# Zero blocks, unread products and small copies moved inside a fused attention and expert kernel

## The chip, the core and the metric

The kernel runs on one core of a Trainium2 chip. The metric is the time of one execution on the device in microseconds (us). Five engines work side by side, each with its own instruction queue in program order: TensorE (PE; its weight loads are listed as PEld), VectorE (DVE), ScalarE (ACT), GpSimd (POOL) and SyncE (SP, which here only issues transfers). They wait for one another and for the transfers (DMA) through semaphores. TensorE writes its results to PSUM, the other tiles lie in SBUF, inputs and outputs in DRAM. The instruction order on each engine is fixed by the order in the source.

## The reference

Two parts, one after the other. First, attention for 8 batches and 8 heads of 64 channels, with 512 local and 32 global tokens: a global token attends to everything, a local token to the 32 global tokens and to the local tokens at most 32 positions away. Then the 8 x 544 = 4352 rows of 512 channels go to a layer of 8 experts, each of which takes at most 80 rows:

```python
logits = x @ w_gate                                   # 4352 x 8
expert_idx = np.argmax(logits, axis=1)
probs = softmax(logits);  gate_w = probs[rows, expert_idx]
out = zeros((4352, 512))
for e in range(8):
    tok_idx = np.where(expert_idx == e)[0]
    if len(tok_idx) > 80:
        tok_idx = the 80 of them with the largest gate_w
    h = np.maximum(x[tok_idx] @ w1[e], 0.0)           # 512 -> 1024
    out[tok_idx] = gate_w[tok_idx, None] * (h @ w2[e])  # 1024 -> 512
```

At most 640 of the 4352 output rows differ from zero, so the kernel writes zeros over the whole output and then scatters the experts' rows into it.

## The kernel before

Attention goes in 16 steps q = 0 to 15, each with four heads of one batch. A step prepares its successors: the loads of step q+4, the casts of q+3, the transposes of q+2, and the scores of q+1. `...` marks cuts; the line numbers in the profile are those of the kernel before.

```python
def T_chunk(q, t, cp=None):                       # transposes of q (t = 0) or k (t = 1)
    T_ps = psT([P, 8, 2, 64], FP16, ...)          # PSUM, two tiles with tag T
    ...                                           # 8 transposes (L299)
    nc.scalar.copy(out=dst, in_=src)              # L307: qkT <- T_ps

def qw_copy(q):                                   # L311: the first 32 queries once more behind the 512,
    nc.vector.tensor_copy(out=qkT[q % 2][:, :, 512:544], in_=qkT[q % 2][:, :, 0:32])

def G_fill(q):                                    # which only this product reads
    g_ps = psS(...)                               # PSUM, two tiles with tag S
    ...  nc.tensor.matmul(..., rhs=qkT[q % 2][:, j, 32:544], ...)

def L_fill(q, j):                                 # local scores: L353, L362 on TensorE
    l_ps = [psS([P, 512], FP32, ...) for hh in range(2)]
    ...
    nc.scalar.activation(out=eL[:], in_=l_ps[hh][:], func=AF.Exp, scale=scale)   # L367

def H_chunk(q, h):                                # weighted values of head h (L409)
    ...
    if h % 2:                                     # the norm of two heads
        nc.vector.reciprocal(out=rec[:], in_=o2[:, :, :, 64])                    # L416
        nc.vector.tensor_tensor(out=s["xn"]..., in0=o2..., in1=rec..., op=ALU.mult)  # L417

def X_chunk(q, j): ...                            # transposes of xn (L447), copy of them to xT (L451, L453)
```

The experts' limit of 80 needs a top-80 per expert. The scores are sorted in groups of batches, 8 values in a step of MAX8 (L580) and MATCH_REPLACE8 (L582) on VectorE. The steps wait in a list `work`; `some(n)` emits n of them, and NS gives how many at three places of step q:

```python
NS = [[1, 1, 1]] * 7 + [[1, 1, 2], [1, 1, 0], [1, 2, 1], [1, 1, 1], [2, 2, 2], [1, 1, 0], [2, 2, 3], [1, 1, 0],
                        [0, 0, 0]]

def zeros(n):                                     # L638: n of 17 blocks of 128 x 1024 zeros to the output
    for _ in range(n):
        if nz[0] < 17:
            nc.sync.dma_start(out=out_z[nz[0]], in_=zt[:]); nz[0] += 1

def warm(n):                                      # n products that nobody reads (L651)
    w_ps = psS([P, 512], FP32, "w_ps")
    for _ in range(n):
        nc.tensor.matmul(out=w_ps[:], lhsT=onesb[:], rhs=w1sb[0][:, 0, 0:512], start=True, stop=True)

for q in range(NQ):
    if 0 < q and q + 4 < NQ: load_qk(q + 4)       # SyncE
    if not first and q + 2 < NQ: load_v(q + 2)    # SyncE
    ...
    G_chunk(q); G_all(q); H_chunk(q, 0); Q_chunk(q)
    T_chunk(q + 2, 0)
    ...
    L_fill(q + 1, 0); mask(q + 1, 0)
    ...                                           # La(pend), regroup(q + 3, 0)
    some(NS[q][0])
    H_chunk(q, 1)
    qw_copy(q + 2)
    ...                                           # Lb1(pend): logits of the batch that is done
    some(NS[q][1])
    L_fill(q + 1, 1)
    T_chunk(q + 2, 1); kO_copy(q + 2)
    H_chunk(q, 2)
    ...                                           # mask(q + 1, 1), Lm(pend), Lb2(pend), Ld(late)
    G_fill(q + 1); Q_fill(q + 1, 0)
    ...                                           # regroup(q + 3, 1)
    H_chunk(q, 3)
    X_chunk(q, 0); Q_fill(q + 1, 1); ...; X_chunk(q, 1)
    some(NS[q][2])
    for i in range(*WS[q:q + 2]): load_w(...)     # expert weights, issued by GpSimd
zeros(4)
...                                               # the last batch's gates, the last steps of the top-80
zeros(17)                                         # the rest: 13 blocks
warm(60)
```

`Ld` writes the normalised rows of a batch to a scratch tensor in DRAM (x_scr), as bf16 pairs with the gate behind them. The end of the kernel finds the row numbers of each expert (idx), gathers the rows, and runs the experts:

```python
nc.vector.tensor_tensor(out=idx[:], ...)                          # L903
for e in range(E):
    nc.gpsimd.indirect_dma_start(out=xg[e][:], in_=x_dram.ap(), ...idx[:, e:e + 1]...)   # L907
load_w(NRES + 3, (2, 3)); load_w(NRES + 4, (0, 1, 2, 3))          # the last weights
warm(16)

def fy(e):
    ...                                                           # y_ps: output products (L936)
    nc.vector.tensor_scalar(out=y[:, 0:DF // 2], in0=y_ps[:, 0:DF // 2], scalar1=g, ...)      # L940
    nc.scalar.activation(out=y[:, DF // 2:], in_=y_ps[:, DF // 2:], func=AF.Copy, scale=g)    # L941
    nc.gpsimd.indirect_dma_start(out=out, ...idx[:, e:e + 1]..., in_=y[:], ...)               # L943

fx(0)                                             # transposes of the gathered rows (L918, L921)
for e in range(E):
    if e + 1 < E: fx(e + 1)
    fh(e)                                         # hidden products (L929), relu on ScalarE (L931)
    if e: fy(e - 1)
fy(E - 1)
```

A scatter waits for every zero block, since both write the output. SyncE issues its transfers in order, and each waits for the one eight places before it.

The softmax here doesn't subtract the row's maximum and nothing guards it: scores larger than these inputs give would overflow.

## Time and profile before

The median of three runs is 263.44 us (263.38 to 263.84).

| | busy us of 263.6 | instructions |
|---|---|---|
| TensorE products | 226.8 | 4025 |
| TensorE weight loads | 157.0 | 4025 |
| GpSimd | 162.0 | 245 |
| VectorE | 158.1 | 462 |
| ScalarE | 135.0 | 237 |

| transfer | count | KB each | us from issue to landing (median) |
|---|---|---|---|
| zero blocks (L638) | 17 | 512 | 11.6 |
| q, k (L156) | 16 + 16 | 512 | 5.7, 5.2 |
| v (L214) | 16 | 512 | 6.6 |
| rows to x_scr (L567) | 8 | 385.5 | 11.4 |

The profile of one execution lists for each instruction when it ran and what ended the idle time before it, in the form `[idle <-releaser]`. Its slices give the granted TensorE clock (PEclk, 1.00 is full speed) and the share of time in which the 16 DMA engines were busy. A chain follows the work that ended last back to the start; "issue" is time in which an engine waited for nothing that the profile shows. Where an engine waits for several semaphores, the profile names the one that came last by its own reckoning, which can be the wrong one. Attention takes the time up to about 186 us, and the end of the kernel, from the last batch's gates to the last scatter, the rest.

### The profile page before, as it was taken

The numbers are of one execution on the slowest core, as the hardware profiler recorded it, in microseconds if no ns is written. First come the engines' busy times: TensorE is split into PE (matmuls) and PEld (weight loads), VectorE is DVE, ScalarE is ACT, GpSimd is POOL, SyncE is SP. The second block draws the span as 40 slices with busy tenths as digits, with TensorE's granted clock in tenths as the row PEclk, the third lists the DMA queues.
The fourth block names the chain that finished last, engine by engine and source line by source line (L and its number), as shares of the span: only waits on it lengthen the run. The fifth ranks groups of instructions, "written<-read, shape, count | busy, mean of one in ns | idle before, by whom it ended". The sixth has DMA issues, their size and how long they took to land.

```text
span 263.6 us, 9572 instructions
## 1 busy us (share of the span) xinstructions
PE 226.8 (86%) x4025; PEld 157.0 (60%) x4025; DVE 158.1 (60%) x462; ACT 135.0 (51%) x237; POOL 162.0 (61%) x245
## 2 busy tenths in 40 slices
PE   6887899999999999998998889998959796599990
PEld 2466676776766767666676667766424352477650
DVE  2765545554853888768478687878979880012220
ACT  3657558695695865868569485461230000033420
POOL 2549795787957869569686788986550005832331
PEclk9999999999999999999999999999999999569996
DMA  7999899995998999989998997987999999999921
GB/s 227 245 302 254 267 259 235 285 199 90 252 257 155 261 146 310 194 185 280 171 262 213 213 212 145 204 145 141 262 277 251 223 281 375 417 323 214 242 85 50
DMA packets 67739, 60.05 MB, mean 228 GB/s; under 512 B 46192, under 2 KB 50544, under 8 KB 67696
## 3 DMA queue, kind: packets, MB, share of 16 engines
q1 hardware_dynamic: 59712, 40.61, 53.6%
q0 software_dynamic: 7840, 18.80, 39.1%
q8 instruction: 31, 0.51, 0.8%
q14 instruction: 12, 0.10, 0.1%
q10 hardware_dynamic: 144, 0.03, 0.1%
HBM read 61.57 MB, written 14.70 MB: 289 GB/s over the span
## 4 chain that ended last, share of the span: by engine, by line
PE 36%; DVE 20%; DMA 18%; issue 9%; ACT 5%; POOL 5%; SPq 3%; POOLq 1%; ACTq 0%; DVEq 0%
DMA out_dram<-zt 10%; PE o_ps L409 8%; DMA x_scr<-xgb 6%; PE o_ps L396 5%; DVE xn L417 5%; PE T_ps L299 4%; PE og L432 4%; PE x_ps L447 4%; DVE scT L582 3%; DVE lst L580 3%; ACT qkT L307 2%; ACT eL L367 2%; POOL out_dram L943 2%; PE l_ps L362 2%; PE lt_ps L472 2%
## 5 line engine op out<-in xcount | busy, mean ns | idle before, releaser
L375 POOL TENSOR_TENSOR eL<-eL,band 128x512 f32<-128x512 f32 x30 | 38.1, 1271 | 27.1 <-ACT eL L367 27.0
L307 ACT COPY qkT<-T_ps 128x1024 f16<-128x1024 f16 x31 | 31.5, 1017 | 33.7 <-PE T_ps L299 28.7
L409 PE MATMUL o_ps<-vb,eL 128*64 128x65 f32 x1024 | 43.7, 227 | 0.0
L367 ACT ACTIVATE eL<-l_ps 128x512 f32<-128x512 f32 x64 | 34.9, 599 | 15.2 <-PE l_ps L362 15.2
L409 PEld LDWEIGHTS o_ps<-vb,eL 128*64 128x64 f32 x1024 | 35.0, 137 | 9.8 <-issue 5.9
L165 ACT CAST qkr<-qkb 128x1024 f16<-128x1024 f32 (+1 forms) x26 | 27.3, 1052 | 2.8 <-DMA qkb<-in_q_l_dram 2.5
L931 ACT ACTIVATE fhT<-h_ps 128x320 bf16<-128x320 f32 x16 | 6.5, 431 | 41.5 <-PE xT_ps L918 38.5
L447 PE MATMUL x_ps<-misc,xn 128*128 128x128 f32 x128 | 20.9, 286 | 7.0 <-DVE xn L417 6.0
L651 PE MATMUL w_ps<-w1sb,onesb 128*128 128x512 bf16 x115 | 26.3, 379 | 0.0
L907 POOL DMA_INDIRECT xg<-x_scr,idx x8 | 7.8, 974 | 26.9 <-DMA out_dram<-zt 24.8
L417 DVE TENSOR_TENSOR xn<-o_ps,rec 128x512 f32<-128x512 f32 x32 | 22.1, 692 | 2.1
L299 PE MATMUL T_ps<-ident,qkr 128*128 128x128 f16 x256 | 20.5, 226 | 1.3 <-ACT qkr L165 1.0
L319 POOL COPY kO<-qkT 128x512 f16<-128x512 f16 x31 | 19.9, 642 | 1.9
L416 DVE RECIPROCAL rec<-o_ps 128x8 f32<-128x8 f32 x32 | 6.5, 203 | 23.1 <-PE o_ps L409 23.1
L447 PEld LDWEIGHTS x_ps<-misc,xn 128*128 128x128 f32 x128 | 13.4, 141 | 10.5 <-DVE xn L417 8.4
L458 POOL CAST xb<-xn 128x1024 bf16<-128x1024 f32 x16 | 16.6, 1040 | 3.8 <-DVE xn L417 3.8
L943 POOL DMA_INDIRECT out_dram<-y,idx x8 | 7.4, 928 | 18.2 <-ACT y L941 9.1
L651 PEld LDWEIGHTS <-onesb 128*128 128x128 bf16 x115 | 10.7, 98 | 13.0 <-issue 1.3
L396 PE MATMUL o_ps<-vg,eG 32*128 32x65 f32 x512 | 18.1, 276 | 0.0
L299 PEld LDWEIGHTS <-qkr 128*128 128x128 f16 x256 | 15.2, 100 | 4.3 <-ACT qkr L165 1.9
L226 POOL COPY vb<-vb 64x1040 f32<-64x1040 f32 x16 | 17.0, 1065 | 0.9
L396 PEld LDWEIGHTS o_ps<-vg,eG 32*128 32x128 f32 x512 | 15.8, 186 | 2.3 <-issue 1.5
(155 smaller groups left out, 473.8 us busy)
## 6 DMA issues: line engine op xcount, KB each, us to landing
out_dram<-zt SPq DMA_DIRECT2D x17, 512.0 KB, 11.6
qkb<-in_q_l_dram SPq DMA_DIRECT2D x16, 512.0 KB, 5.7
qkb<-in_k_l_dram SPq DMA_DIRECT2D x16, 512.0 KB, 5.2
vb<-in_v_l_dram SPq DMA_DIRECT2D x16, 512.0 KB, 6.6
w2sb<-in_moe_w_dram POOLq DMA_DIRECT2D x12, 512.0 KB
w1sb<-in_moe_w_dram POOLq DMA_DIRECT2D x10, 512.0 KB
x_scr<-xb SPq DMA_DIRECT2D x8, 385.5 KB, 11.4
vb<-in_moe_w_dram POOLq DMA_DIRECT2D x6, 512.0 KB
```

The source lines that it names most:

```text
L165: cp(out=qkr[q][:, t, i].rearrange("p i g d -> p g i d"), in_=qkb[q % 2][:, t, :, i])
L226: nc.gpsimd.tensor_copy(out=v[64:128, 1], in_=v[64:128, 0])
L299: nc.tensor.transpose(out=T_ps[:, i].rearrange("x a p -> x (a p)"), in_=qkr[q][:, t, i].rearrange("p g d -> p (g d)"), identity=ident16[:, :])
L307: nc.scalar.copy(out=dst, in_=src)
L319: eng.tensor_copy(out=kO[q % 2][:, a], in_=buf[:, 608:1120].rearrange("x (u w y) -> x u w y", w=2, y=64)[:, :, ::-1, :])
L367: nc.scalar.activation(out=eL[:], in_=l_ps[hh][:], func=AF.Exp, scale=scale)
L375: eng.tensor_tensor(out=eL[:], in0=eL[:], in1=band[:].rearrange("p t i -> p (t i)"), op=ALU.mult)
L396: nc.tensor.matmul(out=s["o"][h][:, u, :], lhsT=s["eG"][32 * r:32 * r + 32, 128 * u:128 * u + 128], rhs=vg[b % 2][32 * r:32 * r + 32, qd, ...
L409: nc.tensor.matmul(out=o[64 * odd:64 * odd + 64, u, :], lhsT=s["eL"][h][:, 64 * t:64 * t + 64], rhs=v[:, 16 * odd + 4 * h + u, :], start=F ...
L417: nc.vector.tensor_tensor(out=s["xn"][:, :, 64 * h - 64:64 * h + 64].rearrange("p u (h d) -> p h u d", h=2), in0=o2[:, :, :, 0:64], in1=re ...
L447: nc.tensor.transpose(out=x_ps[:, 128 * u:128 * u + 128], in_=s["xn"][:, u, 128 * j:128 * j + 128], identity=identf[:, :])
L651: nc.tensor.matmul(out=w_ps[:], lhsT=onesb[:], rhs=w1sb[0][:, 0, 0:512], start=True, stop=True)
```

## The change

The change moves small pieces of work, and the result stays the same row by row.

- Six of the 17 zero blocks are issued one at a time at the end of the steps 3, 4, 5, 8, 12 and 13, so that seven instead of thirteen are left for the end.
- The unread products ahead of the first gathered rows become 27 instead of 16. They keep TensorE at work while it waits.
- The copy of the first 32 queries (`qw_copy`) goes from VectorE to ScalarE, and stands directly behind the copy of the transposed q that it reads.
- In the steps 9 and 11 one top-k step goes from the second place to the third, from before the norm of the last two heads to behind it.
- The last expert's y is scaled by VectorE alone, without ScalarE's half.

```diff
     def qw_copy(q):
-        nc.vector.tensor_copy(out=qkT[q % 2][:, :, 512:544], in_=qkT[q % 2][:, :, 0:32])
+        nc.scalar.copy(out=qkT[q % 2][:, :, 512:544], in_=qkT[q % 2][:, :, 0:32])
...
-    NS = [[1, 1, 1]] * 7 + [[1, 1, 2], [1, 1, 0], [1, 2, 1], [1, 1, 1], [2, 2, 2], [1, 1, 0], [2, 2, 3], [1, 1, 0],
+    NS = [[1, 1, 1]] * 7 + [[1, 1, 2], [1, 1, 0], [1, 1, 2], [1, 1, 1], [2, 1, 3], [1, 1, 0], [2, 2, 3], [1, 1, 0],
...
         elif q + 2 < NQ:
             T_chunk(q + 2, 0)
+            qw_copy(q + 2)
...
         H_chunk(q, 1)
-        if not first and q + 2 < NQ:
-            qw_copy(q + 2)
...
+        if q in (3, 4, 5, 8, 12, 13):
+            zeros(1)
         for i in range(*WS[q:q + 2]):
             load_w(i // 4, (i % 4,))
...
-    warm(16)
+    warm(27)
...
-        nc.vector.tensor_scalar(out=y[:, 0:DF // 2], in0=y_ps[:, 0:DF // 2], scalar1=g, scalar2=None, op0=ALU.mult)
-        nc.scalar.activation(out=y[:, DF // 2:], in_=y_ps[:, DF // 2:], func=AF.Copy, scale=g)
+        n = DF if e == E - 1 else DF // 2
+        nc.vector.tensor_scalar(out=y[:, 0:n], in0=y_ps[:, 0:n], scalar1=g, scalar2=None, op0=ALU.mult)
+        if n < DF:
+            nc.scalar.activation(out=y[:, n:], in_=y_ps[:, n:], func=AF.Copy, scale=g)
```

The cuts leave out the calls for the first steps: `qw_copy(1)` and `qw_copy(2)` move behind their transposes in the same way.

## Prediction

> **What bounds the kernel now.** I read the page first (engine shares, slices, chain), then the chain in order of time, then the timeline of the end and of two attention steps, and last the busy times by window.
>
> The page's chain says that no engine holds the whole span: TensorE carries a third, and DMA, mostly the zero blocks, 18%.
>
> ```profile
> ## 4 chain that ended last, share of the span: by engine, by line
> PE 36%; DVE 20%; DMA 18%; issue 9%; ACT 5%; POOL 5%; SPq 3%; POOLq 1%; ACTq 0%; DVEq 0%
> DMA out_dram<-zt 10%; PE o_ps L409 8%; DMA x_scr<-xgb 6%; PE o_ps L396 5%; DVE xn L417 5%; PE T_ps L299 4%; PE og L432 4%; PE x_ps L447 4%; DVE scT L582 3%; DVE lst L580 3%; ACT qkT L307 2%; ACT eL L367 2%; POOL out_dram L943 2%; PE l_ps L362 2%; PE lt_ps L472 2%
> ```
>
> In order of time the zero blocks are one stretch (start, length, what):
>
> ```profile
> 196.95 15.96 DMA x_scr<-xgb
> 212.92 11.57 DMA out_dram<-zt
> 224.51 15.91 DMA out_dram<-zt
> ```
>
> It ends at 240.42, where the first scatter could go. I don't believe this stretch as the cause of the end. The timeline (start, length, engine, line) shows a second path beside it:
>
> ```profile
> 217.96 3.61 PE L651 MATMUL w_ps<-w1sb,onesb 128*128 128x512 bf16 x16
> 218.34 0.16 DVE L903 TENSOR_TENSOR idx<-idf,inv_ps 80x8 uint32<-80x8 f32 x1
> 219.38 1.04 POOL L907 DMA_INDIRECT xg<-x_scr,idx  x1 [24.78 <-DMA out_dram<-zt]
> ...
> 230.74 0.77 ACT L931 ACTIVATE fhT<-h_ps 128x320 bf16<-128x320 f32 x2 [37.48 <-PE xT_ps L918]
> ...
> 256.50 0.48 DVE L940 TENSOR_SCALAR y<-y_ps,xg 80x256 f32<-80x256 f32 x1 [1.25 <-PE y_ps L936]
> 257.01 0.47 ACT L941 ACTIVATE y<-y_ps,xg 80x256 f32<-80x256 f32 x1 [1.26 <-DVE y L940]
> 257.76 0.92 POOL L943 DMA_INDIRECT out_dram<-y,idx  x1 [0.81 <-ACT y L941]
> ```
>
> The indices are ready at 218.50, the first gather starts 0.88 us later, its rows reach TensorE at 225.77, the first expert's y is scaled at 235.96, the eighth at 256.50, and only 0.28 us after the last y the last scatter starts. Scatters that wait for 240.42 then run every 1.27 us against one y in about 3.0 us, so their backlog is gone by 244 to 247. The end hangs on the experts, not on the zeros. And the experts start on a slow TensorE (window, length, busy times, then PEclk, DMA share, GB/s):
>
> ```profile
> 190.00:195.00 5.00, 2.15 (x10) 0.78 (x8) 4.45 (x24) 2.68 (x9) 3.35 (x8) 1.00 1.05 307
> 222.00:226.00 4.00, 0.23 (x4) 0.24 (x4) 0.00 (x0) 0.00 (x0) 3.06 (x4) 0.81 1.03 416
> 226.00:230.00 4.00, 3.06 (x44) 2.76 (x42) 0.65 (x2) 0.00 (x0) 3.39 (x5) 0.50 1.03 417
> 230.00:234.00 4.00, 2.78 (x34) 2.46 (x34) 0.33 (x1) 1.64 (x4) 3.03 (x5) 0.50 1.04 398
> 234.00:238.00 4.00, 4.00 (x48) 2.67 (x47) 0.71 (x2) 1.17 (x3) 0.00 (x0) 0.91 1.09 249
> ```
>
> The 16 unread products end at 221.57, TensorE stands still until 225.77 (4.2 us), and the clock is halved until about 234.7. In 190:195 there is a pause of 2.9 us (192.15 to 195.07) and the clock stays at 1.00.
>
> In attention, two waits matter here. In an odd step (q=11) ScalarE copies the transposed q (L307), then takes the exponentials whose end frees the PSUM tile of the next products (L353); and DVE, late with the top-k step, delays L447:
>
> ```profile
> 138.69 1.01 ACT L307 COPY qkT<-T_ps 128x1024 f16<-128x1024 f16 x1 [2.43 <-PE T_ps L299]
> 139.64 1.09 ACT L367 ACTIVATE eL<-l_ps 128x512 f32<-128x512 f32 x2
> 140.29 0.38 PE L353 MATMUL l_ps<-bandneg,ident 128*128 128x512 f16 x1
> 142.08 0.83 DVE L311 COPY qkT<-qkT 128x64 f16<-128x64 f16 x1
> 145.06 0.69 DVE L417 TENSOR_TENSOR xn<-o_ps,rec 128x512 f32<-128x512 f32 x1
> 145.81 0.65 PE L447 MATMUL x_ps<-misc,xn 128*128 128x128 f32 x4 [1.27 <-DVE xn L417]
> ```
>
> **What the Trainium skill says.** "TensorE: Matmul & The Clock Gate", section "What's actually happening": after at least one idle window of about 3.4 us the clock goes to half, and about 3.4 us of sustained work bring it back; the window runs freely. The trace agrees: 4.2 us of pause gave 0.50, 2.9 us did not. "DMA: Bandwidth & Descriptors", section "Issuing engines are not separate DMA queues": transfers of all issuers interleave on the same 16 engines. The trace agrees: the first gather, 80 rows, took 6.4 us from its start to its use while zeros and weights moved 400 to 417 GB/s. "GPSIMD Engine Reference", section "1. Specifications": its SBUF interface is shared with VectorE, with contention in two-port modes. That fits L311, one small copy that takes between 0.17 and 1.00 us (median 0.375).
>
> **The change, part by part.**
>
> Unread products, 16 to 27. One costs 3.61/16 = 0.226 us, so 27 take 6.1 us and end at 224.06 instead of 221.57 on today's time axis. The pause before 225.77 shrinks from 4.2 to 1.7 us, under the 2.9 us that was harmless, so I expect the clock to stay at 1.00. They don't delay the gathered rows, which come at 225.8 or at best some 1.5 us sooner. At full clock the start of the experts is: products of expert 0 1.31 us, transposes of expert 2 0.31, then the pair "hidden products of expert 1, output of expert 0", which in steady state takes 238.98 - 235.90 = 3.08 us. From 226.63 that is 231.3, against 235.96 now. Gain 4.6 us; I take 4.4.
>
> Six zero blocks moved. Each is 0.524 MB. At 410 GB/s that is 1.28 us, six are 7.7 us of DMA work that leaves the end, so the zeros end near 233 instead of 240. By the argument above this alone doesn't move the end. It may shorten the first gather's 6.4 us; but of the thirteen late blocks it is the last six that go; nine are issued before 220, and seven of them stay, so I take 0.5 us. In attention the blocks meet DMA engines that show a share of 0.92 (60 to 120 us) to 0.97 (120 to 170), but 207 to 213 GB/s against 417 at the end, and loads that land 5.2 to 6.6 us after issue and are read about one step (11 us) later. Cost there: 0.
>
> The last y on VectorE alone. Now 0.48 on DVE and 0.47 on ScalarE one after the other, 256.50 to 257.48. A DVE evacuation of 512 columns from PSUM (L453) takes 0.68. I take 0.73 with the scale: gain 0.25.
>
> The wrap copy on ScalarE. DVE loses 16 copies of 0.375 us. ScalarE gets one between L307 and L367. Its smallest operation in the trace (128x40) takes 0.25 us; it must wait for L307 to end, which costs the 0.08 us by which L367 starts before L307's end now, and 0.04 to start. That shifts L367 by 0.29 us. In odd steps the shift goes straight to L353 (140.29 waits for the first exponential), in even steps to the copy of the logits, for which TensorE waits up to 0.5 us now. Thirteen steps have it: at most 13 x 0.29 = 3.8 us; not every shift will reach the end of its step, I count 8, cost 2.3 us. On DVE the copy is off the path except in q=8, where it holds a PSUM tile back by 0.14 us.
>
> The two top-k steps. In q=9 and q=11 one step of MAX8 and MATCH_REPLACE8 (1.16 and 0.90 us) goes from before the norm of the last heads to behind it. TensorE waits there 1.03 and 1.27 us, where the other steps wait 0.32 to 0.33. The last heads' products end at 121.75 and 143.81; norm (0.2 + 0.7) and starts put L447 at 122.85 and 144.93 instead of 123.51 and 145.81: gains of 0.66 and 0.88.
>
> Sum: 263.44 - 4.4 - 0.5 - 0.25 + 2.3 - 0.14 - 0.66 - 0.88 = 258.9 us.
>
> **Rivals.** (1) The clock falls all the same. For: the window runs freely, transposes and the wait for the second gather follow the unread products, and if the gather is late the pause grows. Against: 1.7 us is far from 3.4. Then only 0.5 + 0.25 + 1.7 - 2.3 remain: 263.3 us. (2) ScalarE becomes the bound of attention: all 13 shifts count, 260.4 us. For: L307, L367, the regrouping casts and L342 run without a gap in an odd step. (3) The wrap copy is absorbed, and freeing DVE and its shared port helps GpSimd too: 256.6 us. For: the spread of L311. Against: GpSimd waits for ScalarE in these steps (27.0 us at L375), not for the port. (4) The zeros delay loads of attention: the blocks stand ahead of loads in SyncE's order, and SyncE has a wait of 1.9 us on such a chain already. Each late load would cost 1 to 3 us: 260 to 264 us. (5) The late weights of experts 6 and 7, issued behind the gathers, become the wait when the experts run 4.6 us sooner. Against: they have no zeros beside them then.
>
> **Range and chances.** The clock term is the surest large one; attention can be off by 2 us either way, and the cadence after y0 holds one irregular step (3.90 against 3.0 us) that I leave as it is. So 258.9 us, 255.5 to 262.3. Two per cent is 258.2, just under my figure: faster by over 2% 0.42, within 2% 0.56, slower 0.02.
>
> **What would show it.** Right: PEclk of 1.00 from the first gathered rows on, the first y about 11.7 us after the first gather starts (16.6 - 4.4 - 0.5) instead of 16.6, the zeros' last landing before the first y. Wrong if: PEclk shows 0.5 there (rival 1); attention ends (the last L417, now 185.03) more than 2.5 us later (2, or 4 if ScalarE's cast L165 waits for DMA) or earlier than now (3); TensorE waits for w1sb or w2sb among the experts (5).

## The result, and the profile after

The changed kernel takes 266.91 us (266.71 to 267.32), against 263.41 us for the kernel before on the same chip: a ratio of 1.0137, interval 1.0112 to 1.0162. It is 3.5 us slower. The prediction was 258.9 us, and its range ended at 262.3.

In the changed kernel all lines behind L844 have moved by two: the gather is L909, the relu L933, y L943 and L945, the scatter L947. Its page gives this chain (shares of the span):

```profile
PE 36%; DMA 22%; ACT 11%; issue 10%; POOL 9%; DVE 6%; SPq 3%; POOLq 1%; ACTq 0%
PE o_ps L409 8%; DMA out_dram<-zt 6%; PE o_ps L396 6%; PE T_ps L299 5%; DMA x_scr<-gate 5%; ACT qkT L307 5%; PE og L432 4%; DMA vg<-in_v_g_dram 4%; ACT eL L367 3%; DMA x_scr<-xb 3%; PE x_ps L447 3%; DVE xn L417 3%; POOL out_dram L947 2%; PE l_ps L362 2%; POOL xg L909 2%
```

VectorE's share has fallen from 20% to 6% and ScalarE's has risen from 5% to 11%, as the moved copy and top-k steps would make it. Two transfers are new among the lines listed, the gate behind the rows of the last batch (x_scr<-gate, 5%) and the values of the global tokens (vg, 4%). In order of time (start, length, what) the first of them stands here:

```profile
188.68 5.04 DMA x_scr<-xgb
193.74 16.95 DMA out_dram<-zt
210.71 12.63 DMA x_scr<-gate
223.58 0.61 issue
```

The gate write of the last batch is issued at 210.71, 22 us after attention's last norm (188.64), where it was 17 us before (202.14 after 185.03); it lands at 223.34, and the first gather starts 1.07 us behind that. The timeline of the end (start, length, engine, line) shows what that costs:

```profile
222.23 0.16 DVE L905 TENSOR_TENSOR idx<-idf,inv_ps 80x8 uint32<-80x8 f32 x1
224.41 1.04 POOL L909 DMA_INDIRECT xg<-x_scr,idx  x1 [26.21 <-DMA out_dram<-zt]
...
230.22 0.32 PE L920 MATMUL xT_ps<-identbf,xg 80*128 80x80 bf16 x4 [2.38 <-DMA xg<-x_scr,idx]
...
231.58 0.45 PE L920 MATMUL xT_ps<-identbf,xg 80*128 80x80 bf16 x4 [1.04 <-DMA xg<-x_scr,idx]
...
233.19 0.44 ACT L933 ACTIVATE fhT<-h_ps 128x320 bf16<-128x320 f32 x1 [36.32 <-PE h_ps L931]
...
258.66 0.75 DVE L943 TENSOR_SCALAR y<-y_ps,xg 80x512 f32<-80x512 f32 x1 [1.25 <-PE y_ps L938]
259.69 0.91 POOL L947 DMA_INDIRECT out_dram<-y,idx  x1 [0.58 <-DVE y L943]
```

The gather starts 2.02 us behind the row numbers instead of 0.88. The pause of TensorE ahead of the first rows is 2.4 us instead of 4.2, and a wait of 1.0 us for the second rows follows. And the clock falls all the same (window, length, busy times, then PEclk, DMA share, GB/s; the first line is the kernel before, the others are the changed one):

```profile
200.00:205.00 5.00, 5.00 (x25) 2.27 (x24) 4.76 (x12) 0.00 (x0) 0.00 (x0) 1.00 1.11 237
...
200.00:205.00 5.00, 5.00 (x18) 1.86 (x16) 4.76 (x14) 0.00 (x0) 0.00 (x0) 0.66 1.06 272
...
226.00:230.00 4.00, 1.84 (x9) 0.63 (x7) 0.00 (x0) 0.00 (x0) 3.08 (x4) 1.00 1.04 421
230.00:234.00 4.00, 2.74 (x41) 2.61 (x42) 0.65 (x2) 0.44 (x1) 3.08 (x4) 0.59 0.72 260
234.00:238.00 4.00, 4.00 (x44) 3.16 (x42) 0.32 (x1) 1.31 (x3) 4.00 (x7) 0.56 0.70 120
```

The first two lines stand behind the pause of 2.9 us for the gates that the prediction used as its measure. In the kernel before it left the clock at 1.00; here the same pause, again 2.92 us, halves it (0.50 from 200 to 203 us).

In attention, ScalarE's timeline of step 11 shows the copy (L311) where the change puts it:

```profile
143.19 1.01 ACT L307 COPY qkT<-T_ps 128x1024 f16<-128x1024 f16 x1 [2.41 <-PE T_ps L299]
144.23 0.24 ACT L311 COPY qkT<-qkT 128x64 f16<-128x64 f16 x1
144.38 1.08 ACT L367 ACTIVATE eL<-l_ps 128x512 f32<-128x512 f32 x2
145.35 1.05 ACT L165 CAST qkr<-qkb 128x1024 f16<-128x1024 f32 x1
```

The exponentials start 1.19 us behind the start of L307, where it was 0.95 before (139.64 - 138.69): 0.24 us later.

Last, SyncE's queue around the block of step 5, first in the changed kernel:

```profile
80.29 5.90 SPq L567 DMA_DIRECT2D x_scr<-xb  x1
...
90.28 0.42 SPq L638 DMA_DIRECT2D out_dram<-zt  x1
92.45 0.39 SPq L156 DMA_DIRECT2D qkb<-in_q_l_dram  x1
94.55 0.38 SPq L156 DMA_DIRECT2D qkb<-in_k_l_dram  x1
95.02 0.43 SPq L214 DMA_DIRECT2D vb<-in_v_l_dram  x1
95.50 4.54 SPq L218 DMA_DIRECT2D vg<-in_v_g_dram  x2
```

and then in the same kernel without the six moved blocks (e7 below):

```profile
86.34 0.63 SPq L214 DMA_DIRECT2D vb<-in_v_l_dram  x1
87.03 8.73 SPq L218 DMA_DIRECT2D vg<-in_v_g_dram  x4
```

A row write alone takes 5.90 us to issue here, but 5.87 us in e7 as well. What differs is the wait for places in the queue: of the 172 transfers in this trace none starts before the one eight places ahead has landed, and the loads at 92.45 and 94.55 start 0.07 us behind two writes of rows (L568 and L569, issued at 86.24 and 86.76) that landed 6.1 and 7.7 us after their issue. So the values are asked for 8.5 us later than without the blocks, though the step itself is only 2.5 us later (start of L396 in step 7: 94.74 against 92.23). They land at 105.28, and TensorE starts step 8 with them at 105.33.

Besides the global scores, which the text above the prediction names alone, the last tile of the local scores (L362) also reads the wrap copy (its columns are 480 to 544). It changes nothing in the argument.

### The profile page after: what moved, and what is told of

Same layout as the page of the kernel before. It is cut to its first block, busy times and chain, and to the rows that moved or that the text cites. A ratio compares the mean times of both kernels' runs of the same rounds, so it can differ in the third digit from the quotient of the medians.

```text
span 265.5 us, 9521 instructions
## 1 busy us (share of the span) xinstructions
PE 232.2 (87%) x4036; PEld 159.9 (60%) x4036; DVE 151.0 (57%) x446; ACT 137.5 (52%) x252; POOL 161.1 (61%) x245
## 4 chain that ended last, share of the span: by engine, by line
PE 36%; DMA 22%; ACT 11%; issue 10%; POOL 9%; DVE 6%; SPq 3%; POOLq 1%; ACTq 0%
PE o_ps L409 8%; DMA out_dram<-zt 6%; PE o_ps L396 6%; PE T_ps L299 5%; DMA x_scr<-gate 5%; ACT qkT L307 5%; PE og L432 4%; DMA vg<-in_v_g_dram 4%; ACT eL L367 3%; DMA x_scr<-xb 3%; PE x_ps L447 3%; DVE xn L417 3%; POOL out_dram L947 2%; PE l_ps L362 2%; POOL xg L909 2%
## 5 line engine op out<-in xcount | busy, mean ns | idle before, releaser
L307 ACT COPY qkT<-T_ps 128x1024 f16<-128x1024 f16 x31 | 31.5, 1017 | 34.5 <-PE T_ps L299 29.3
L409 PE MATMUL o_ps<-vb,eL 128*64 128x65 f32 x1024 | 44.8, 230 | 1.3 <-issue 1.3
L367 ACT ACTIVATE eL<-l_ps 128x512 f32<-128x512 f32 x64 | 34.7, 594 | 17.1 <-PE l_ps L362 17.1
L409 PEld LDWEIGHTS o_ps<-vb,eL 128*64 128x64 f32 x1024 | 35.9, 140 | 11.3 <-issue 7.3
L651 PE MATMUL w_ps<-w1sb,onesb 128*128 128x512 bf16 x126 | 30.4, 396 | 0.0
L933 ACT ACTIVATE fhT<-h_ps 128x320 bf16<-128x320 f32 x16 | 6.7, 430 | 38.4 <-PE h_ps L931 38.4
L909 POOL DMA_INDIRECT xg<-x_scr,idx x8 | 7.8, 972 | 28.3 <-DMA out_dram<-zt 26.2
L299 PE MATMUL T_ps<-ident,qkr 128*128 128x128 f16 x256 | 19.9, 221 | 2.9 <-DVE qkr L165 1.6
L651 PEld LDWEIGHTS <-onesb 128*128 128x128 bf16 x126 | 12.2, 101 | 15.6 <-issue 3.6
L319 POOL COPY kO<-qkT 128x512 f16<-128x512 f16 x31 | 19.1, 616 | 1.9
L396 PE MATMUL o_ps<-vg,eG 32*128 32x65 f32 x512 | 19.1, 282 | 0.1
L458 POOL CAST xb<-xn 128x1024 bf16<-128x1024 f32 x16 | 16.6, 1039 | 3.2 <-DVE scT L582 2.4
L396 PEld LDWEIGHTS o_ps<-vg,eG 32*128 32x128 f32 x512 | 16.9, 191 | 2.5 <-issue 1.5
L299 PEld LDWEIGHTS <-qkr 128*128 128x128 f16 x256 | 14.4, 98 | 6.2 <-ACT qkr L165 2.1
L947 POOL DMA_INDIRECT out_dram<-y,idx x8 | 7.4, 925 | 15.2 <-ACT y L945 14.6
```

The costliest lines, as they stand in the source:

```text
L299: nc.tensor.transpose(out=T_ps[:, i].rearrange("x a p -> x (a p)"), in_=qkr[q][:, t, i].rearrange("p g d -> p (g d)"), identity=ident16[:, :])
L319: eng.tensor_copy(out=kO[q % 2][:, a], in_=buf[:, 608:1120].rearrange("x (u w y) -> x u w y", w=2, y=64)[:, :, ::-1, :])
L396: nc.tensor.matmul(out=s["o"][h][:, u, :], lhsT=s["eG"][32 * r:32 * r + 32, 128 * u:128 * u + 128], rhs=vg[b % 2][32 * r:32 * r + 32, qd, ...
L409: nc.tensor.matmul(out=o[64 * odd:64 * odd + 64, u, :], lhsT=s["eL"][h][:, 64 * t:64 * t + 64], rhs=v[:, 16 * odd + 4 * h + u, :], start=F ...
```

## The experiments

Each run has the kernel before beside it on its own chip; its median there was 264.0 us (e1 to e4), 264.4 (e6 to e9), 268.2 (e10 to e14), 267.4 (e15 to e18) and 267.2 (e19, e20). The ratios leave out disturbed executions and the medians don't, so the ratios decide.

Three lengths carry the verdicts, all from the timelines of the profiled runs. *Late* is by how much the steps 1 to 14 of attention, from one start of L396 to the next, exceed the shortest lengths that the runs with the same place of the wrap copy and of the top-k steps show (for e2 and e8, each alone of its kind, taken step by step from the nearest such runs). *Relu* is the time from the first hidden product to the first relu. *First y* is the time from the start of the first gather to the first y.

| run | what differs from before | ratio to before (interval) | late us | gather to rows | relu | first y |
|---|---|---|---|---|---|---|
| before | | | 0.3 | 6.4 | 4.1 | 16.6 |
| after | all of the change | 1.0137 (1.0112 to 1.0162) | 1.4 | 5.8 | 1.4 | 14.5 |
| e1 | 27 products | 1.0011 (0.9979 to 1.0043) | 0.4 | 6.4 | 1.0 | 13.2 |
| e2 | wrap copy | 1.0001 (0.9966 to 1.0037) | 2.2 | 6.5 | 1.4 | 13.6 |
| e3 | zero blocks | 270.8 us, no interval | 7.5 | 6.5 | 1.4 | 13.8 |
| e4 | top-k steps | 0.9917 (0.9884 to 0.9950) | 0.8 | 6.6 | 1.4 | 13.2 |
| e6 | after, wrap copy undone | 267.4 us, no interval | 6.5 | 5.8 | 1.4 | 13.1 |
| e7 | after, zero blocks undone | 1.0022 (0.9993 to 1.0051) | 1.5 | 6.5 | 0.9 | 13.3 |
| e8 | wrap copy, end of step | 0.9932 (0.9895 to 0.9969) | 2.3 | 6.5 | 1.4 | 13.2 |
| e9 | steps, last y, 36 products | 0.9996 (0.9949 to 1.0043) | 3.1 | 6.4 | 0.8 | 11.6 |
| e10 | e9 and e8 | 0.9953 (0.9916 to 0.9989) | 6.3 | 6.4 | 4.0 | 16.8 |
| e11 | e10, 3 zero blocks, 8 y buffers | 0.9897 (0.9785 to 1.0010) | 7.1 | 6.4 | 4.1 | 16.7 |
| e13 | after, 36 products | 1.0310 (1.0209 to 1.0410) | 6.1 | 6.4 | 4.1 | 16.9 |
| e14 | after, 4 blocks later | 1.0005 (0.9953 to 1.0057) | 4.4 | 6.7 | 4.2 | 17.9 |
| e15 | steps, e8, last y, 8 y buffers | 0.9874 (0.9772 to 0.9975) | 0.4 | 6.4 | 4.0 | 17.6 |
| e16 | after, blocks by GpSimd | 1.0074 (1.0017 to 1.0132) | 3.0 | 6.3 | 4.3 | 16.3 |
| e17 | 13 zero blocks left out | 0.9916 (0.9877 to 0.9955) | 1.1 | 2.6 | 3.0 | 15.7 |
| e18 | 36 products | 1.0030 (0.9996 to 1.0064) | 1.6 | 6.4 | 4.0 | 16.7 |
| e19 | e15, 6 blocks behind gathers | 0.9761 (0.9650 to 0.9873) | 4.8 | 6.4 | 1.4 | 14.8 |
| e20 | e15 once more | 0.9891 (0.9759 to 1.0023) | 0.9 | 6.7 | 3.9 | 17.7 |

### One part alone: e1 to e4

Four runs put one part of the change each into the kernel before. Their edits are those of the change: 27 unread products (e1); the wrap copy on ScalarE behind L307 (e2); the six zero blocks in steps 3, 4, 5, 8, 12 and 13 (e3); the two top-k steps behind the norm (e4).

```diff
-    warm(16)
+    warm(27)                                                     # e1
-        nc.vector.tensor_copy(out=qkT[q % 2][:, :, 512:544], ...)
+        nc.scalar.copy(out=qkT[q % 2][:, :, 512:544], ...)       # e2, behind T_chunk(q + 2, 0)
+        if q in (3, 4, 5, 8, 12, 13): zeros(1)                   # e3
-    ... [1, 2, 1], [1, 1, 1], [2, 2, 2] ...
+    ... [1, 1, 2], [1, 1, 1], [2, 1, 3] ...                      # e4
```

Expected of e1, on record:

> The kernel before with one change: 27 unread products instead of 16 ahead of the gathered rows. Theory A (the count is right, and the changed kernel lost it only because its rows came 4.5 us later): rows at about 225.8, products end at about 224.0, clock 1.00 from 226 on, first y near 231.5 instead of 235.96, time about 259. Theory B (transposes and the wait for the second gather count as a pause too, so the clock falls all the same): clock near 0.5 until 234, first y near 236, time 263.4.

Measured: 264.81 us, ratio 1.0011. The eleven products more bring nothing, and the clock falls in spite of them: the pause ahead of the rows is 1.9 us in the profiled run, and PEclk is 0.57 from 230 to 234. The profiled run shows the first y 13.2 us after the gather, but so do e4 and e8 with 16 products.

Expected of e2:

> The kernel before with the wrap copy alone moved to ScalarE, directly behind the copy of the transposed q. Theory A (it stands in front of the exponentials that free the PSUM tile, so each of the steps 1 to 13 grows by 0.20 to 0.28 us): attention ends 2.8 to 3.5 us later, time 266 to 267. Theory B (the zero blocks lengthened the steps, not the copy): 263.4, or less since VectorE is freed.

Measured: 264.74 us, ratio 1.0001. By steps it is plain what the copy does: 0.21 to 0.29 us more in each of the steps 1 to 7, 10, 12 and 13 (step 5, late in this run, is taken from e7), nothing in 8 and 14, and 0.35 and 0.72 us less in 9 and 11, where VectorE was late. A loss and a gain lie on top of one another (+2.4 and -1.1 us in attention). The interval allows a loss of 1.0 us at most, so the sum of 1.3 us is a little more than the times show.

Expected of e3:

> The kernel before with six zero blocks alone moved into the steps 3, 4, 5, 8, 12 and 13. Theory A (the DMA engines have no room there; the blocks push later transfers back, so that the last rows of x_scr land after the indices are ready): steps as before but for one late load near step 8, last write of x_scr lands 3 us or more after the 212.9 of before, first gather starts up to 1 us later; time 263.4 to 265. Theory B (the blocks are free in attention): gather starts as before, lands up to 1.5 us sooner, time 262 to 263.4.

Measured: 270.6 to 272.3 us in three executions and 265.0 in the fourth, so the size of the loss stays open. The profile of one of the three shows where time can go. The waits of TensorE in 140 to 156 us (engine, what it waited for, us in total, times, longest):

```profile
PE o_ps L396 <- DMA vg<-in_v_g_dram: 3.0, 1, 3.0
```

and the chain in this stretch:

```profile
141.61 10.21 DMA vg<-in_v_g_dram
151.86 2.46 PE o_ps L396 x30
```

The same L396 takes 1.05 us elsewhere. The wait for the late values stops TensorE for 3.0 us, and the clock is 0.50 from 152 to 158 behind it: one late load is paid twice, once as a wait and once as a slower TensorE. Steps 11 and 12 together are 5.4 us longer for it.

Expected of e4:

> The kernel before with the two top-k steps alone moved behind the norm. Theory A (VectorE was late there): step 9 shorter by 0.66, step 11 by 0.88 us, attention ends 1.5 us sooner, time 261.9. Theory B (VectorE is late all the same, since its wrap copy still stands there): less than half of that, 262.7 to 263.4.

Measured: 261.45 us, ratio 0.9917, faster. Step 9 is 0.71 us shorter and step 11 0.93, against the predicted 0.66 and 0.88.

### One part of the changed kernel undone: e6, e7

e6 is the changed kernel with the wrap copy on VectorE again, e7 the changed kernel without the zero blocks in attention.

```diff
-        nc.scalar.copy(out=qkT[q % 2][:, :, 512:544], ...)
+        nc.vector.tensor_copy(out=qkT[q % 2][:, :, 512:544], ...) # e6, at its old place
-        if q in (3, 4, 5, 8, 12, 13): zeros(1)                    # e7
```

> The changed kernel with the wrap copy back on VectorE; everything else of the change stays. Theory A (the moved zero blocks are what makes the changed kernel slow: they hold back SyncE's queue, so attention's loads of v and the last gate write come late): it stays slower than the kernel before, 264 to 268 us, and TensorE's waits for vg or vb and a gate write issued later than 205 us are still there. Theory B (the copy on ScalarE is the main loss, 0.2 to 0.3 us in each ordinary step): with it gone the two top-k steps (1.6 us) and the last y remain as gains, 260 to 262 us.

> The changed kernel without the six zero blocks in attention; 13 are left for the end as in the kernel before. Theory A (the zero blocks make the loss): 261.5 to 264 us, the first gather again 0.9 us after the row numbers, the gate write issued within 17.2 us of attention's last norm; the copy on ScalarE and the two top-k steps nearly cancel in attention. Theory B (the copy on ScalarE makes the loss): as slow as the changed kernel, 265.5 to 268 us.

Measured: e6 266.5 to 268.7 us in three executions and 261.1 in the fourth; e7 263.92 us, ratio 1.0022. Three executions of e6 lie where theory A puts them and one where theory B does, so e6 doesn't decide. e7 does: without the zero blocks alone the loss is gone. That is theory A. The ratios 1.0137 and 1.0022 put the price of the six blocks at 0.0115 x 263.4 = 3.0 us (some 1 us either way by the two intervals, and the two were measured on different chips). In e6 the first gather starts 5.1 us behind the row numbers, later still than in the changed kernel, and the last gate write is issued later too, 25.2 us behind attention's last norm (213.57 against 188.40). In e7 it is 19.7 us, later than the 17.2 expected; in the profiled runs that move no block it is 17.1 to 20.5.

Of these 3.0 us the profiled execution of the changed kernel shows only a part: 1.1 us at the gate, and 0.7 us in the steps 7 and 8 around the vg loads. Its steps as a whole run no later than those of e7 (1.4 us against 1.5). The rest is shown by the times alone.

### The place of the copy: e8

```diff
-    def qw_copy(q):
+    def qw_copy(q, cp=nc.vector.tensor_copy):
-        nc.vector.tensor_copy(out=qkT[q % 2][:, :, 512:544], ...)
+        cp(out=qkT[q % 2][:, :, 512:544], ...)
...
+        if not first and q + 2 < NQ:                              # end of step q, behind X_chunk(q, 1)
+            qw_copy(q + 2, nc.scalar.copy)
         some(NS[q][2])
```

> The kernel before with the wrap copy on ScalarE, but at the end of the step, where ScalarE stands idle for about 2.5 us before the next copy of the transposed q; nothing else is changed. Theory 'place' (what costs is that the copy stands between L307 and the exponentials L367): the ordinary steps are as long as before (10.0 and 11.3 us) and the steps 9 and 11, where VectorE was late, still lose 0.35 and 0.7 us: 262.0 to 262.8 us. Theory 'engine' (ScalarE is full in a step and any copy more lengthens it): each ordinary step is 0.2 to 0.3 us longer again, 263.2 to 264.5 us.

Measured: 261.26 us, ratio 0.9932, faster than before. ScalarE's timeline in it:

```profile
137.20 0.30 ACT L311 COPY qkT<-qkT 128x64 f16<-128x64 f16 x1
139.76 1.01 ACT L307 COPY qkT<-T_ps 128x1024 f16<-128x1024 f16 x1 [2.26 <-PE T_ps L299]
140.69 1.08 ACT L367 ACTIVATE eL<-l_ps 128x512 f32<-128x512 f32 x2
```

The copy sits in the gap before L307, which still waits 2.26 us for its transposes, and L367 follows L307 after 0.93 us as in the kernel before. The ordinary steps are as long as before (10.0 and 11.3 us) and step 11 keeps its gain. The place costs, not the engine.

### More products, and what stands behind them: e9, e10, e13, e18

e9 has the two top-k steps, the last y on VectorE and 36 unread products; e10 has the late wrap copy as well. e13 is the changed kernel with 36 products, e18 the kernel before with 36.

```diff
-    warm(16)
+    warm(36)                                                      # e9, e10, e18; e13: 27 to 36
```

> The kernel before with the two top-k steps moved, the last y on VectorE alone, and 36 unread products in place of 16, which end about when the first gathered rows are there. Theory 'pause' (the clock falls because TensorE stands still before the first rows; a pause filled wholly keeps it at 1.00): PEclk 1.00 from the gather to the experts, the first y about 12 us after the first gather starts, 257 to 259.5 us. Rival 'thin work' (transposes and the wait for the second gathered rows are enough for the clock to fall): the clock falls to 0.5 to 0.6 behind the first transposes, the first y 13.2 us or more after the gather, 260 to 261.5 us, as with the steps alone.

> The kernel before with the gains alone: the two top-k steps moved, the wrap copy on ScalarE at the end of the step, the last y on VectorE, 36 unread products; no zero block moved. Theory 'end bound by zeros and late weights' (with 36 products the experts start 4 us sooner and then run into the late weights and into y tiles whose scatter waited for the zero blocks): attention's last norm at about 182.8 us, from there to the last scatter 69.5 us as with 36 products before, 259.5 to 261 us in all; TensorE waits about 1 us for w1sb or w2sb of the last expert and VectorE 4 to 5 us for a scatter. Rival 'end bound by the experts alone': no such waits, 33 us from the row numbers to the last scatter instead of 35.7, 257 to 258.5 us.

> The changed kernel with 36 unread products instead of 27. Theory 'pause': the products now end when the first gathered rows are there, PEclk stays at 1.00, the first y comes 11.6 to 12.2 us after the first gather instead of 14.5, 264 to 265 us. Rival 'the clock falls on thin work behind the products, whatever their number': PEclk 0.5 to 0.6 for about 4 us behind the first transposes again, 266 to 267.5 us.

> The kernel before with 36 unread products instead of 16 and nothing else. Theory 'the pause before the first rows is what halves the clock': PEclk 1.00 until the experts, the first y 11.6 to 12 us after the first gather, ratio 0.985 to 0.995. Rival 'stall': TensorE, VectorE and ScalarE stand for about 3 us behind the first hidden products, whatever the number of unread products, and the clock falls behind that: the first y 16 to 17 us after the gather, ratio 0.998 to 1.003.

Measured: ratios 0.9996, 0.9953, 1.0310, 1.0030. Only e9 shows what the prediction had hoped for. Its windows at the start of the experts:

```profile
226.00:230.00 4.00, 3.58 (x69) 2.76 (x67) 0.97 (x3) 0.87 (x2) 3.08 (x4) 1.00 1.03 415
230.00:234.00 4.00, 4.00 (x67) 2.99 (x64) 0.71 (x2) 1.86 (x5) 4.00 (x7) 1.00 1.03 414
```

The clock stays at 1.00, and the first y comes 11.6 us after the gather; the prediction had 11.7. And then the gain is given back:

```profile
227.18 0.31 PE L918 MATMUL xT_ps<-identbf,xg 80*128 80x80 bf16 x4
...
243.61 0.98 POOL L945 DMA_INDIRECT out_dram<-y,idx  x1 [9.18 <-ACT fhT L931]
...
247.78 1.27 PE L929 MATMUL h_ps<-fxT,w1sb 128*128 128x80 bf16 x30 [0.17 <-DMA w1sb<-in_moe_w_dram]
...
252.69 1.02 PE L936 MATMUL y_ps<-w2sb,fhT 128*80 128x512 bf16 x4 [1.05 <-DMA w2sb<-in_moe_w_dram]
253.19 1.37 DVE L941 TENSOR_SCALAR y<-y_ps,xg 80x256 f32<-80x256 f32 x2 [5.13 <-DMA out_dram<-y,idx]
...
255.66 0.91 POOL L945 DMA_INDIRECT out_dram<-y,idx  x1 [0.30 <-issue]
```

TensorE waits 0.17 and 1.05 us for the weights of the last expert: that is the fifth rival. But another wait sets the end. y has six buffers, so the seventh y needs the first scatter to have landed. That scatter starts at 243.61, 1.15 us behind the landing of the last zero block (242.46), and lands 9.45 us later, at 253.06; the products of the seventh y are ready at 250.78 and stand until 253.19. With the late weights alone the last scatter could have started at about 254.7 instead of 255.66 (an estimate: the last products end at 253.71, and the changed kernel takes 0.75 us for the last y and 0.28 us from it to the scatter). The kernels with 16 products that have no stall end in the same way. In e8:

```profile
243.17 0.98 POOL L943 DMA_INDIRECT out_dram<-y,idx  x1 [9.98 <-ACT fhT L931]
...
252.28 1.06 DVE L940 TENSOR_SCALAR y<-y_ps,xg 80x256 f32<-80x256 f32 x2 [3.90 <-DMA out_dram<-y,idx]
```

From attention's last norm to the last scatter e9 takes 69.5 us, e4 69.8 and e8 69.7. The experts start sooner in e9, and the zero blocks, through the first scatter, still set when they end.

In e10, e13 and e18 the pause ahead of the rows is closed too, and the first y still comes 16.7 to 16.9 us after the gather. In e18 (same columns):

```profile
226.00:230.00 4.00, 3.29 (x49) 2.27 (x48) 0.65 (x2) 0.00 (x0) 2.98 (x4) 1.00 1.03 417
230.00:234.00 4.00, 1.45 (x20) 1.17 (x20) 0.33 (x1) 0.77 (x2) 4.00 (x7) 0.89 1.02 412
```

From 230 to 233 the clock is still at 1.00, and TensorE is busy for 1.45 of the 4 us of the second window. The first relu comes 4.0 us behind its products instead of 0.8. TensorE, VectorE and ScalarE stand together for some 2 to 3 us while GpSimd goes on, and the clock falls only behind that (0.55 from 233 on). This stall, not the pause, is the larger part of the slow start that the prediction saw in the kernel before: its relu, at 230.74, came 4.1 us after the products at 226.63. e13's profile adds 6.1 us of late steps to the stall, but so does that of e10 (6.3 us); why e13 is the slowest stays open.

### The zero blocks: e11, e14, e16, e17

e11 puts three blocks into steps 3, 4 and 5 of e10 and gives y eight buffers. e14 is the changed kernel with the four blocks behind attention moved behind the gate write. e16 is the changed kernel with the six blocks issued by GpSimd. e17 is the kernel before without the last thirteen blocks; those output rows are left unwritten, so its time is only a measure.

```diff
+        if q in (3, 4, 5): zeros(1)                               # e11
-        y = rpool.tile([cap, DF], FP32, tag="y", bufs=6, ...)
+        y = rpool.tile([cap, DF], FP32, tag="y", bufs=8, ...)     # e11
-    zeros(4)                                                      # e14: then eleven at the end
-            zeros(1)
+            nc.gpsimd.dma_start(out=out_z[nz[0]], in_=zt[:])      # e16
+            nz[0] += 1                                            # e16
-    zeros(17)                                                     # e17
```

> The same, and three zero blocks go into attention at the end of the steps 3, 4 and 5, and the y tiles have eight buffers in place of six. Theory 'end bound by zeros and late weights': three blocks of 1.28 us fewer at the end bring the weights 3.8 us sooner, no wait of TensorE for w1sb or w2sb and none of VectorE for a scatter is left, 33 us from the row numbers to the last scatter: 2.5 us less than without. Theory 'any zero block in attention delays a load': attention is 2 to 5 us longer, and the sum is 259 to 263 us. If both hold, they cancel; the step lengths 3 to 8 and the waits for vg and vb tell.

> The changed kernel without the four zero blocks that stand between attention and the last batch's row writes; they are written with the three others at the end (eleven then). Theory 'queue' (these four hold SyncE's next writes, so that the last gate write is issued 22 us behind attention's last norm and the first gather waits for it): the gate write is issued within 17.5 us of the last norm, the first gather starts 0.9 us behind the row numbers instead of 2.0, 1.1 us less than the changed kernel: 265 to 266 us. Rival (the delay comes from the blocks in the steps 12 and 13 and the row writes behind them): the gate write stays late, 266.5 to 267.5 us.

> The changed kernel with its six zero blocks of attention issued by GpSimd at the same places instead of SyncE; all else as in the changed kernel. Theory 'queue' (the blocks do harm because SyncE issues in order and waits for the transfer eight places before, so loads of v and vg and the row writes behind a block are issued late): TensorE's waits for vg are gone or under 0.5 us, no step is over 0.6 us longer than without moved blocks, ratio to the kernel before 0.995 to 1.005. Rival 'traffic' (the DMA engines are full in attention, and 0.5 MB more delays the loads whichever engine issues it): waits of 1 to 3 us for vg or v again, ratio 1.01 or more.

> The kernel before without the thirteen zero blocks of the end (those output rows are left unwritten; the four blocks behind attention stay). It measures what the zero blocks cost at the end. Theory 'contention': the first gather's rows come 3 to 4.5 us after its start instead of 6.4, the first scatter starts right behind the first y, and the end is 2 to 3.5 us shorter: 260 to 261.5 us. Rival (the gather takes its time by itself and the zeros are hidden beside it): 6.0 to 6.4 us from the gather to its rows, 262.5 to 263.5 us.

e11: ratio 0.9897, an interval that reaches 1. Steps 7 and 8 are 2.8 and 3.2 us longer around a wait of 2.0 us for vg. It looks as if three blocks were enough to make a load late, but e10, the same kernel without them, waits for vg too (2.1 us in three pieces). Whether three blocks fewer at the end free the late weights can't be read from it: the stall made the experts start so late in this execution, and in e10, that no weight was waited for by TensorE in the last ones.

e14: ratio 1.0005. The gate write is issued 13.2 us behind the last norm, and the first gather starts 0.9 us behind the row numbers, as it should. But in e13, which keeps the four blocks, it did so too; so a late gate is a matter of the single execution, and the run doesn't settle which blocks make it late. Nor does the time: against the changed kernel it is 3.5 us (some 1.5 us either way) where 1.1 were expected, so the whole loss is gone although the six blocks are still in attention. The chip is another one, and e13 lies at 1.0310 on it. The 3.0 us above are therefore the price of the blocks in one pair of kernels, not a fixed price.

e16: ratio 1.0074, between the two expectations. TensorE has no wait for vg, though these loads land up to 10.5 us after issue (9.8 in the changed kernel): they are slow here too, but asked for in time they come in time. Two steps (7 and 14) are 1.1 and 1.6 us longer, without a wait for a load; in both TensorE shows a gap with "issue" ahead of it (0.9 and 0.8 us). That fits theory 'queue' and doesn't prove it: e13 and e14, whose blocks SyncE issues, have no wait for vg in their profiles either, the changed kernel has one of 0.3 us, and the interval of the ratio meets that of the changed kernel. What the 0.7% is stays open.

e17: the first gather and what follows (timeline, cut):

```profile
220.60 1.04 POOL L906 DMA_INDIRECT xg<-x_scr,idx  x1 [26.28 <-DVE idx L902]
...
223.22 0.32 PE L917 MATMUL xT_ps<-identbf,xg 80*128 80x80 bf16 x4 [0.43 <-DMA xg<-x_scr,idx]
...
227.73 0.44 ACT L930 ACTIVATE fhT<-h_ps 128x320 bf16<-128x320 f32 x1 [34.75 <-PE xT_ps L917]
228.22 1.21 PE L928 MATMUL h_ps<-fxT,w1sb 128*128 128x80 bf16 x16 [2.06 <-issue]
...
231.99 0.77 ACT L930 ACTIVATE fhT<-h_ps 128x320 bf16<-128x320 f32 x2 [3.82 <-remote]
232.05 0.33 DVE L920 COPY fxT<-xT_ps 128x320 bf16<-128x320 bf16 x1 [6.83 <-remote]
```

The rows arrive 2.6 us after the gather starts instead of 6.4: the zero blocks cost the gather 3.8 us. Most of that is lost again. The engines stand twice, released by "issue" and "remote", that is by nothing that the profile lists. The DMA share in 226 to 230 is 0.25, so it isn't the traffic that makes them stand. The kernel gains 0.8%, 2.2 us.

### What is left when only the gains are kept: e15, e19, e20

e15 has the top-k steps, the late wrap copy, the last y on VectorE and eight y buffers, with 16 products and no moved zero block. e20 is e15 once more, beside e19, which has six of the last zero blocks issued by GpSimd between the fourth gather and the fifth.

```diff
-    zeros(17)
+    zeros(7)
...
     for e in range(E):
         nc.gpsimd.indirect_dma_start(out=xg[e][:], ...)
+        if e == 3:
+            for i in range(nz[0], 17):
+                nc.gpsimd.dma_start(out=out_z[i], in_=zt[:])      # e19
```

> The kernel before with the two top-k steps moved, the wrap copy on ScalarE at the end of the step, the last y on VectorE alone, eight buffers for y, and no change to unread products (16) or zero blocks. Theory: the gains of attention hold without the rest of the change and need no fix of the clock; attention's last norm at about 183 us, ratio to the kernel before 0.985 to 0.992 (259.5 to 261.3 us against 263.4). Rival (what attention gains the end gives back, since it waits for zero blocks and late weights): ratio 0.995 or more.

> The kernel with the top-k steps, the late wrap copy on ScalarE, the last y on VectorE and eight y buffers, and the last six zero blocks issued by GpSimd between the fourth and the fifth gather instead of by SyncE ahead of them. Theory: fewer blocks stand ahead of the first gather, its rows come in 2.6 to 5 us instead of 6.4, and the first y comes as much sooner; against this the late weights are issued 4 us later and the last two experts may wait for them. Net 0 to 2 us better than the same kernel without held blocks. Rival: the weights or the zero blocks behind the gathers end the kernel, 1 to 3 us worse.

> The same kernel without the held blocks, once more, as the measure for the run with them: ratio to the kernel before 0.985 to 0.992. If it is 0.995 or more, the gain of attention does not last to the end.

Measured: e15 0.9874, e20 0.9891, e19 0.9761. All three lie below the kernel before and well below the changed kernel (the interval of e20 just reaches 1.002). e19 has the lowest ratio, though its interval meets the other two. It isn't so for the reason expected:

```profile
223.07 1.04 POOL L907 DMA_INDIRECT xg<-x_scr,idx  x1 [25.35 <-DMA out_dram<-zt]
...
227.92 3.27 POOL L912 DMA_DIRECT2D out_dram<-zt  x6
...
229.45 0.45 PE L921 MATMUL xT_ps<-identbf,xg 80*128 80x80 bf16 x4 [4.18 <-DMA xg<-x_scr,idx]
```

The rows still take 6.4 us. With seven blocks ahead of it instead of thirteen the gather is no sooner; with none (e17) it is. That fits what the Trainium skill says in "DMA: Bandwidth & Descriptors", section "Queues, rings and completion order", that each DMA engine takes turns between the queues it has work for, a packet at a time. Then the gather shares the engines as long as any zero block is under way, and how many wait behind it doesn't matter. The turns themselves are in no trace here. Why e19 is ahead of e20 stays open; its profiled run lacks the stall behind the first products, which e20's has.

## Why the prediction was wrong

**The sum, term by term.** In us, as predicted and as the runs show it:

| term | predicted | measured | from |
|---|---|---|---|
| 27 products keep the clock | -4.4 | 0 (-0.6 to +1.1) | e1 |
| first gather sooner | -0.5 | part of the next line | after |
| zero blocks in attention | 0 | +3.0 (2.0 to 4.0) | after against e7 |
| wrap copy, ordinary steps | +2.3 | +2.4 to 2.8 | e2, e7 |
| wrap copy, q = 8 | -0.14 | 0 | e2 |
| top-k steps | -1.54 | -1.64 | e4 |
| last y | -0.25 | -0.23 | after |

With the measured terms the sum is 263.4 + 3.0 + 2.6 - 1.6 - 0.2 = 267.2 us, and the kernel takes 266.9. As the 3.0 comes from the changed kernel itself, this tests the small terms alone. They were right, that of the wrap copy partly by luck: 8 shifts of 0.29 us were counted, and 10 to 12 of 0.2 to 0.3 came. The clock and the zero blocks were wrong.

**The clock.** The step that failed is "under the 2.9 us that was harmless, so I expect the clock to stay at 1.00". It made one execution's pause a bound. The prediction had quoted the Trainium skill for a window that runs freely, and the changed kernel fits that, though the window itself is in no trace here: the same pause of 2.92 us halves the clock there. In e1 the pause ahead of the rows is 1.9 us, close to the 1.7 predicted, and the clock falls behind it (0.57 from 230 to 234). In e7 a pause of 1.95 us was enough, with only 0.97 us of work in the 2 us from 228 to 230 (clock 0.52 and 0.62 from 230 to 234). So rival 1 came true, by the sign that was named for it; its time of 263.3 us lacked the zero blocks.

**The size of the clock term.** "231.3, against 235.96 now" took all of the start's slowness for the clock. About 2.7 us of it (a relu after 4.1 us instead of 1.4) is the stall of three engines, which was in the profile of before at 230.74, and was overlooked there. There was a warning: the profiled execution took 265.4 us, 2.0 us more than the median of the timed ones. What is really to be had from a clock at 1.00 is 13.2 - 11.6 = 1.6 us (e4 and e8 against e9), and the end takes it back: there the zero blocks, the first scatter behind them and the six buffers of y decide.

**The zero blocks in attention.** "Cost there: 0" failed, because it weighed each load's landing (5.2 to 6.6 us, a step ahead of its use) and not its issue. Rival 4 named the mechanism: a block stands ahead of loads in SyncE's order. With the queue eight deep, its lateness is handed on to the vg loads (asked for 6 us late in step 7 of the changed kernel, 8.5 less the step's own 2.5), from there to TensorE's start of a step, and in e3 to the clock behind that. How much of the 3.0 us this chain makes is argued and not shown. In the 13 profiled runs without moved blocks (before, e1, e2, e4, e7 to e10, e15, e17 to e20) the steps 1 to 14 are 2.0 us late on average, in the six with blocks moved on SyncE (after, e3, e6, e11, e13, e14) 5.5 us. That is no clean count, since steps run late by 4 us and more in two of the 13 as well (e10, e19), and the changed kernel itself is late by only 1.4 us; the difference of 3.5 us is of the size of the 3.0 us, no more. Rival 4's time of 260 to 264 us was too low only because it still held the 4.4 us of the clock.

**The first gather.** "I take 0.5 us" for six blocks fewer: the way was right and the size unknown. All blocks gone are worth 3.8 us in the landing (e17), six gone 0.6 us in the changed kernel (5.81 against 6.39) and next to nothing in e19 (6.38 against 6.41 and 6.66). The new wait for the gate, 1.1 us in the profiled run, wasn't thought of.

**The rest.** Rival 2 is out: the wrap copy costs what was counted, and attention's last norm is 3.6 us later in the profile, out of which 0.7 us are the copy less the top-k steps, 1.2 us late steps, and 1.75 us the load and step 0, where the clock fell in this execution (so it did in e1, e2 and e15, without zero blocks). Rival 3 is out, in step 8 too. Rival 5, the late weights, shows when the experts really start sooner (1.05 us in e9), but the wait that sets the end there was in no rival: the seventh y waits for the first scatter, and that one for the zero blocks. "The end hangs on the experts, not on the zeros" holds in the kernel before, whose last scatter starts 0.28 us behind the last y. It fails in e4, e8 and e9, where the first y comes 3.3 to 5.0 us sooner behind the gather.

**What stays open.** What the stall behind the first products is. It is in all eight profiled runs of two of the chips (e10 to e18) and in none of the eight of two others (e1 to e9); 16, 27 or 36 products don't matter, and traffic isn't needed (e17). The medians of the kernel before are higher on the two chips with the stall (268.2 and 267.4 us against 264.0 and 264.4), as they would be if it had the stall there too; then a ratio from these chips holds a stall on both sides, and ratios from different chips compare badly. Shorter gaps of 1.2 to 2.4 us with the same mark ("issue", nothing listed) occur in attention in the changed kernel and in e3, e6, e8 and e14. The page lists queues "instruction" with 31 and 12 packets among the transfers, but none of these falls into the stall in the kernel before (from 229.2 to 230.7; the nearest are at 221.1 and 234.5) or in e18 (from 229.8 to 232.5; at 222.7 and 236.6). A wait for such a packet is not what these two show.

## What to carry to other kernels

A bulk transfer put into a "free" place of an in-order issue queue can delay what is issued behind it (8.5 us for the vg loads here); look at when the next small loads are issued, and not only at how long they take to land. Before a stage is sped up, ask which buffers its end needs: six y tiles and a first scatter behind the zero blocks took back what a full clock had gained. A short operation is free on an engine only at a place where that engine waits: the same copy cost 0.24 us a step between two links of a chain and nothing 2.6 us ahead of it. And before a gain is read from one profile, compare that execution's time with the median of the timed ones, and don't turn one pause that left the clock alone into a bound.

## What the runs showed of the hardware

- A pause of TensorE of 2.92 us left the clock at 1.00 in one execution and halved it for more than 3 us in another; one of 1.95 us with thin work behind it halved it too (e7). The Trainium skill, "TensorE: Matmul & The Clock Gate", section "What's actually happening", says that the window is free-running; its idle window of about 3.4 us is no safe bound here.
- A gather of 80 rows reaches TensorE in 2.6 us on quiet DMA engines, and in 5.8 to 6.7 us while zero blocks are under way, whether seven or thirteen of them are left.
- Three engines can stand together for 2 us and more (TensorE 2.06 us in e17, with the DMA engines at a share of 0.25), while GpSimd works on.
- A wait of 3.0 us for 64 KB of values (four loads of 16 KB) cost an attention step more than its own length (e3): the next matmuls took 2.46 us instead of 1.05, on a clock of 0.50.
- The first scatter of 80 rows behind the zero blocks landed 9.0 to 9.5 us after its issue (e4, e8, e9), the last one 2.6 us after it.
